# A weight conversion's negative step on GpSimd instead of ScalarE, and eight times it added on VectorE

## The chip, the core and the metric

The kernel runs on one core of a Trainium2 chip. The metric is the device time of one execution in microseconds (us); several runs are given by their median. Below, PE is TensorE, DVE is VectorE, ACT is ScalarE, POOL is GpSimd and SP is the engine that issues nearly all DMAs.

## The reference, cut to what matters

The program is an RWKV-6 attention block (4 batches, 8 heads, 768 tokens, head width 48) whose output goes through an MLP mixer. Only the mixer's four weights matter for this change:

```python
h = np.maximum(xt @ w_tok1, 0.0) @ w_tok2
u = x + h.transpose(0, 2, 1)
h2 = np.maximum(u @ w_ch1, 0.0) @ w_ch2
return (u + h2).astype(np.float32)
```

They are handed to the kernel as 64-bit words (the host only views them as such and lays them out), and the kernel makes float32 numbers of them from the 16-bit pieces of each word: it has to turn the top 16 bits into a power of two with its sign, and multiply the rest of the word by it.

## The kernel before

**Stages.** The work begins with the first batch's attention in three units (0, 1, 2; each covers 256 tokens of all heads), while the weights are loaded and converted. Then comes the first batch's mixer: the token product (`hidden`, L947), its way back (`back`, L958), turning x (`turn`, L969), the channel products `up` (L993) and `down` (L1004). The other three batches follow with their attention laid between the matmuls of the mixers.

**What orders the work.** Up to the first `back`, the order is written out by hand in one call of `strict` (L1094 to L1109). After that, `interleaved` merges streams of pieces by the string `ORDER`. `strict` chains the instructions of PE, DVE, ACT and SP, each engine in the order written. POOL is not chained: its instructions stand in the order in which the program made them, and each starts when its semaphores allow. Each engine works through its instructions in order, so one that waits holds up all behind it.

**The conversion.** There are twelve conversions, three of the token weights (`to_tok`; t0, t1, t2 below) and nine of the channel weights (`to_ch`; c0 to c8). Each takes 1024 words per partition, in seven steps that `convert` (L252) makes:

- `load` (L261): a DMA brings the words into one of four rooms (`raw`, `xT`, `z`).
- `positive` (L264), ACT: max(0, 8·top − 114688) over `top`, the highest 16 bits of each word, read with a step of four 16-bit numbers; written as int16 into `plus`.
- `negative` (L267), ACT: max(0, −8·top − 114688) into `minus`.
- `lead` (L270), DVE: `plus − minus`, a `tensor_sub` of two int16 tiles.
- `raise_two` (L273), DVE: the exponent's bits of that, into `minus` again.
- `put` (L277), DVE: rest of the word times the power of two, into the weights.
- `add` (L281), DVE: adds the leading part.

`plus` and `minus` lie in one of three pairs of rooms, so a later conversion's `minus` must wait for the `put` that reads the earlier one. All these tiles lie in SBUF.

**Around it.** The hand-written order puts conversions between the attention's steps. On DVE these are `ends` (L435, a scan), `begins` (L443, a scan), `keys` (L440), `queries` (L446), `own_put` (L458, reads PSUM) and `mask` (L327, a `copy_predicated` of PSUM data). On PE the third unit's `after` (L401) reads what its `mask` wrote. On ACT are the copies of states by the decay (L501), the range flags (L427), the attention's output copies (L407) and the copies of the turned x (L971). POOL makes a few constants at the start, and from the second batch on adds tiles of the mixer (L765).

Of the kernel before, what the change touches and what calls it, by code (L numbers as in the profile page):

```python
# [18 lines left out]
ALU = mybir.AluOpType  # L19
AF = mybir.ActivationFunctionType  # L20
# [6 lines left out]
UB = C // UC  # L27
NU = B * UB
A = H // 2
# [18 lines left out]
SHRINK = (1.0 - 1.0 / BASE) ** 2  # L48
LEAST, MOST = 2.0 ** -40, 2.0 ** 40
MID = 3 * G // 4 * SEG1  # L50
ORDER = (
    "888008088078808800000888484440800840804080880808804844088488400448088408008888080080884808884040488844488888084840880880"
    "808840880808084448484008800080858808005000458500505588854545558485085848785005080558505855588400558085800005606068606846"
# [12 lines left out]
def rwkv6_then_mixer(  # L66
# [25 lines left out]
    def behind(gate, f):  # L92

        def g():
            done = len(block.instructions)
            f()
            tc.add_manual_dep(block.instructions[done], ended[gate], wait, reason="time of issue")

        return g

    def strict(*fs):

        for f in fs:
# [82 lines left out]
    def load_part(i, n):  # L186
        for rows in (slice(0, 128),) if i < UB else (slice(0, D), slice(P, P + D)):
            sp.dma_start(rk_of(i)[rows, ts(n, COLS)], rk[i, n, rows, :])

    def load_rk(i):  # L190
        if i < NU:
            for n in (1, 0):
                load_part(i, n)
# [3 lines left out]
    def load_v(i):  # L197
        if i < NU:
            vs[i] = vpool.tile([128, UC, DM], f32, name="vt", tag=f"vt{i % 2}")
            b, j = divmod(i, UB)  # L200
            sp.dma_start(vs[i], v[b, ts(j, UC * 128), :].rearrange("(c p) e -> p c e", p=128))
# [50 lines left out]
    def convert(to, words, raw, room):  # L252

        word = raw_words[raw]
        rest = word.rearrange("p (n two) -> p n two", two=2)[:, :, 0]
        top = word.bitcast(i16).rearrange("p (n four) -> p n four", four=4)[:, :, 2]
        plus, minus = parts[room]
        leading, power = plus.bitcast(bf16), minus.bitcast(bf16)

        def load():  # L260
            sp.dma_start(word.bitcast(u16)[:, :words.shape[1]], words)  # L261

        def positive():
            act.activation(plus, top, AF.Relu, bias=rebias, scale=8.0)  # L264

        def negative():
            act.activation(minus, top, AF.Relu, bias=rebias, scale=-8.0)  # L267

        def lead():
            dve.tensor_sub(plus, plus, minus)  # L270

        def raise_two():
            dve.tensor_scalar(minus.bitcast(u16), plus.bitcast(u16), 0xFF80, None, op0=ALU.bitwise_and)  # L273

        def put():
            for dst, cols in to:
                dve.scalar_tensor_tensor(dst, rest[:, cols], 2.0 ** -36, power[:, cols], op0=ALU.mult, op1=ALU.mult)  # L277

        def add():
            for dst, cols in to:  # L280
                dve.tensor_add(dst, dst, leading[:, cols])  # L281

        return load, positive, negative, lead, raise_two, put, add
# [125 lines left out]
    def unit(i):  # L409
# [123 lines left out]
        def each(f, n):  # L533
            return [lambda m=m: f(m) for m in range(n)]

        return dict(ranges=each(ranges, 2), ends=ends, keys=keys, begins=begins, queries=queries, own_u=each(own_u, A),
                    own_gram=own_gram, copied=each(copied, UC), taken=each(taken, 3),
                    own_put=own_put, products=[lambda n=n: products(n) for n in range(3)], sums_put=sums_put,
                    tokens=tokens, gram=gram, mask=mask, carry=carry, before=before, seen=seen, after=after,
# [478 lines left out]
    def attention_pieces(i):  # L1018
# [6 lines left out]
        def piece(f, name, *ops):  # L1025
            return (i, name), f, ops
# [10 lines left out]
        loads = piece(lambda: load_rk(i + 1), "loads", ("Q", 8.0, last("before", "gram", "tokens")))  # L1037
        ends = piece(e["ends"], "ends", ("DVE", 2.6, last("small", "large", "by3", "w")))
        keys = piece(e["keys"], "keys", ("DVE", 1.25, k("ends") + last("loads")))
        small, large = (piece(e["ranges"][n], name, ("ACT", 1.4, k("ends"))) for n, name in enumerate(("small", "large")))  # L1040
        begins = piece(e["begins"], "begins", ("DVE", 2.35, k("ends")))
        tokens = piece(e["tokens"], "tokens", ("PE", 0.9, k("keys") + last("carry"), "k0", "k1"))
        copied = [piece(e["copied"][n], f"copied{n}", ("ACT", 0.6, k("tokens")), ("free", f"k{n}")) for n in range(2)]
# [31 lines left out]
    def interleaved(order, *streams):  # L1075
# [9 lines left out]
    raw_words.append(turned["xT"].rearrange("p m t -> p (m t)").bitcast(u32)[:, :4 * PIECE])  # L1085
    to_tok = conversion(("wtok1", "wtok2"), words_tok, rooms=lambda n: ((0, 1, 3)[n], n % 2))
    to_ch = conversion(("wch1", "wch2"), words_ch, rooms=lambda n: (n % 2, n % 2) if n else (2, 2))
    e0, e1, e2 = (unit(i) for i in range(UB))
    (_, p0, n0, lead0, two0, put0, add0), (_, p1, n1, lead1, two1, put1, add1), (_, p2, n2, lead2, two2, put2, add2) = to_tok
    _, p3, n3, lead3, two3, put3, _ = to_ch[0]  # L1090
    in_turn.update({pe.engine: None, dve.engine: None, act.engine: None, sp.engine: None})
    s0, s1, s2 = (e["updates"] for e in (e0, e1, e2))
    t0, t1, t2 = (e["scaled"] for e in (e0, e1, e2))
    strict(lambda: load_part(0, 1), masks, e0["ends"], e0["own_u"][0], e0["own_u"][1], e0["own_u"][2], e0["own_u"][3], e0["begins"],  # L1094
           lambda: load_part(0, 0), e0["keys"], lambda: load_part(1, 1), e0["own_gram"], lambda: load_v(0), e0["ranges"][0], lambda: load_w(1),
           e0["tokens"], e0["queries"], e1["own_u"][0], e1["own_u"][1], e0["copied"][0], lambda: load_w(2), e0["gram"], e1["ends"], e0["copied"][1],
           lambda: load_part(1, 0), e0["carry"], e1["own_u"][2], s0[0], e0["own_put"], e1["own_u"][3], e0["ranges"][1], t0[1], s0[1],
           behind(e0["tokens"], to_tok[0][0]), e1["begins"], behind(e1["ends"], lambda: load_part(2, 1)), e1["own_gram"], t0[2], e1["keys"],
           e2["own_u"][0], s0[2], e2["own_u"][1], e1["own_put"], t0[3], e1["tokens"], behind(e0["tokens"], lambda: load_part(2, 0)),
           e0["before"], e2["own_u"][2], e0["mask"], e1["copied"][0], p0, e0["seen"], s0[3], e2["own_u"][3], behind(t0[2], lambda: load_v(1)),  # L1100
           e2["ends"], e1["copied"][1], t1[0], e0["after"], e0["taken"][0], e1["carry"], n0, to_tok[1][0], s1[0], e1["queries"], e0["taken"][1],
           e2["keys"], lead0, t1[1], e2["own_gram"], two0, s1[1], e0["taken"][2], e2["own_put"], e2["tokens"], t1[2], put0, e2["copied"][0],
           s1[2], t1[3], e2["copied"][1], e1["gram"], s1[3], e1["before"], t2[0], p1, add0, lambda: load_v(2), e1["mask"], e2["carry"], e1["seen"],
           h[1], s2[0], h[0], e2["ranges"][0], e2["begins"], behind(t1[1], to_tok[2][0]), t2[1], n1, h[3], e2["queries"], s2[1], lead1, two1,
           e1["after"], t2[2], s2[2], put1, e2["gram"], behind(e1["gram"], to_ch[0][0]), h[2], e1["taken"][0], e1["taken"][1], t2[3], e1["taken"][2],
           behind(t2[3], lambda: load_w(3)), p2, add1, e2["mask"], lambda: load_v(UB), behind(e2["own_gram"], to_ch[1][0]), e2["before"], h[4],
           e2["seen"], n2, e2["after"], lead2, two2, h[5], e2["taken"][0], h[6], e2["taken"][1], put2, e2["taken"][2], h[7], h[8], p3,
           h[10], add2, n3, behind(e1["tokens"], to_ch[2][0]), lead3, two3, rectified[0], h[9], h[11], rectified[1], e1["ranges"][0], e2["ranges"][1], e1["ranges"][1],
           lambda: load_rk(3), put3, lambda: turned["back"](0))  # L1109

    six_banks.close()
    ps_g, ps_m = None, six_banks.enter_context(tc.tile_pool(name="ps_m", bufs=1, space=bass.MemoryType.PSUM))
# [2 lines left out]
    def single(steps, n):  # L1115

        load, positive, negative, lead, raise_two, put, add = steps
        k = lambda *names: tuple(("to", n, name) for name in names)
        last = lambda back, *names: tuple(("to", n - back, name) for name in names) if n > back else ()
        whole = [("load", load, ("Q", 5.0, last(2, "value", "minus"))), ("plus", positive, ("ACT", 1.15, k("load") + last(2, "put"))),  # L1120
                 ("minus", negative, ("ACT", 1.15, k("load") + last(2, "value"))), ("lead", lead, ("DVE", 0.69, k("plus", "minus"))),
                 ("two", raise_two, ("DVE", 0.35, k("lead"))), ("value", put, ("DVE", 1.23, k("two"))), ("put", add, ("DVE", 1.23, k("value")))]
        return [(("to", n, name), f, (op,)) for name, f, op in (whole[-1:] if n == 0 else whole[1:] if n <= 2 else whole)]

# [221 lines left out]
```

## Time and profile before

| | us |
|---|---|
| median of 3 runs | 479.33 (477.25 to 480.75) |
| the profiled execution | 478.31 |
| its span in the trace | 476.5 |

The profiled execution is 1.81 us longer than its span: that is what lies around the span. PE is busy for 459.1 us of the span, DVE for 344.6, ACT for 265.8 and POOL for 54.2. A row of a timeline gives the start and the length in us, the engine, the line, the operation, the tiles as out<-in with partitions x elements and types, the number of merged instructions, and in brackets the idle time before it with what ended it. A row that groups instructions gives the shortest, the median and the longest in ns. Busy time on an engine says what it did, not what the end of the program waited for; the chain of waits says that.

### The profile page before, as it was taken

How to read it: one execution, taken by the hardware profiler on the slowest of the kernel's cores; microseconds unless marked ns; L12 is line 12 of the kernel's file. 1: busy time of each engine (PE TensorE's matmuls, PEld its weight loads, DVE VectorE, ACT ScalarE, POOL GpSimd, SP SyncE). 2: the span in 40 equal slices, each digit the busy share in tenths (PEclk: the TensorE clock that was granted, in tenths of full speed). 3: DMA queues.
4: the chain of work that ended last, by engine and by line, in shares of the span. 5: the costliest groups of instructions: out<-in, count | busy, mean ns of one | idle time of the engine just before them, and what ended most of it. 6: DMA issues, size and time to landing. Idle time of an engine off the chain costs nothing.

```text
span 476.5 us, 12778 instructions
## 1 busy us (share of the span) xinstructions
PE 459.1 (96%) x5322; PEld 409.6 (86%) x5322; DVE 344.6 (72%) x495; ACT 265.8 (56%) x606; POOL 54.2 (11%) x58
## 2 busy tenths in 40 slices
PE   3899999999999999999999999999999999999996
PEld 2776588856797668999999999999999999999995
DVE  7998797679598877876897998685587885235341
ACT  6699876674678856453747385351837554134140
POOL 1000000000000001231302002130304003032130
PEclk9999999999999999999999999999999999999999
DMA  8865745573584556963888842754784513336331
GB/s 313 317 221 217 188 169 191 180 275 99 152 228 138 177 179 207 284 186 100 252 283 232 294 154 56 198 173 141 215 227 150 167 61 84 115 101 199 86 99 54
DMA packets 45055, 85.34 MB, mean 179 GB/s; under 512 B 4736, under 2 KB 37376, under 8 KB 44992
## 3 DMA queue, kind: packets, MB, share of 16 engines
q1 hardware_dynamic: 44704, 84.37, 56.3%
q8 instruction: 43, 0.70, 0.6%
q14 instruction: 20, 0.16, 0.1%
q10 hardware_dynamic: 288, 0.10, 0.1%
HBM read 72.65 MB, written 11.80 MB: 177 GB/s over the span
## 4 chain that ended last, share of the span: by engine, by line
PE 90%; ACT 4%; DVE 2%; DMA 2%; issue 1%; SPq 0%; DVEq 0%; ACTq 0%
PE bank L1004 10%; PE bank L772 8%; PE bank L779 8%; PE bank L774 8%; PE bank L790 8%; PE bank L792 8%; PE bank L791 8%; PE bank L993 7%; PE bank L667 3%; PE bank L989 3%; PE bank L726 3%; PE bank L315 2%; PE bank L401 2%; PE bank L380 2%; PE kv_ps L365 2%; PE bank L669 2%
## 5 line engine op out<-in xcount | busy, mean ns | idle before, releaser
L765 POOL TENSOR_TENSOR z_high<-z_high 128x384 fp32r<-128x384 f32 x48 | 52.9, 1107 | 406.7 <-DMA ring<-third 186.8
L754 ACT ACTIVATE z_high<-bank 128x384 fp32r<-128x384 f32 x48 | 23.5, 489 | 58.1 <-PE bank L779 57.7
L772 PE MATMUL bank<-x_forms,forms 128*128 128x384 f32 x216 | 50.3, 341 | 0.0
L779 PE MATMUL bank<-z_more,forms 128*128 128x384 f32 x216 | 50.1, 340 | 0.0
L774 PE MATMUL bank<-x_forms,ring 128*128 128x384 f32 x216 | 49.3, 337 | 0.0
L761 DVE SCALAR_TENSOR_TENSOR z_high<-bank,z_high 128x384 fp32r<-128x384 f32 x48 | 26.5, 554 | 31.4 <-ACT z_high L754 29.4
L1004 PE MATMUL bank<-wch,z 128*128 128x384 f32 x144 | 48.1, 488 | 0.0
L790 PE MATMUL bank<-forms,z_high 128*128 128x384 f32 x140 | 47.8, 342 | 0.0
L792 PE MATMUL bank<-forms,z_high 128*128 128x384 f32 x140 | 47.1, 337 | 0.0
L791 PE MATMUL bank<-ring,z_high 128*128 128x384 f32 x140 | 47.1, 337 | 0.0
L798 DVE SCALAR_TENSOR_TENSOR x<-bank,x 128x384 f32<-128x384 f32 x35 | 18.8, 553 | 39.0 <-PE bank L792 38.9
L1004 PEld LDWEIGHTS bank<-wch,z 128*128 128x128 f32 x144 | 26.8, 190 | 17.2
L501 ACT ACTIVATE before<-state,to_end 112x48 f32<-112x48 f32 x132 | 33.1, 324 | 13.0 <-DVE state L516 7.6
L779 PEld LDWEIGHTS bank<-z_more,forms 128*128 128x128 f32 x216 | 39.0, 188 | 0.1
L772 PEld LDWEIGHTS bank<-x_forms,forms 128*128 128x128 f32 x216 | 38.3, 188 | 0.5
L774 PEld LDWEIGHTS bank<-x_forms,ring 128*128 128x128 f32 x216 | 38.6, 188 | 0.0
L993 PE MATMUL bank<-xT,wch 128*128 128x256 f32 x144 | 32.0, 381 | 0.0
L993 PEld LDWEIGHTS bank<-xT,wch 128*128 128x128 f32 x144 | 27.0, 190 | 3.7
L757 ACT ACTIVATE z_high<-z_high 128x384 fp32r<-128x384 f32 x48 | 25.2, 525 | 3.5
L790 PEld LDWEIGHTS bank<-forms,z_high 128*128 128x128 f32 x140 | 26.3, 188 | 0.2
L791 PEld LDWEIGHTS bank<-ring,z_high 128*128 128x128 f32 x140 | 26.3, 188 | 0.0
L792 PEld LDWEIGHTS bank<-forms,z_high 128*128 128x128 f32 x140 | 26.3, 188 | 0.0
(243 smaller groups left out, 961.2 us busy)
## 6 DMA issues: line engine op xcount, KB each, us to landing
ring<-third SPq DMA_DIRECT2D x144, 192.0 KB, 3.4
raw<-in_words_ch_dram SPq DMA_DIRECT2D x8, 1023.8 KB, 4.8
rk<-in_rk_dram SPq DMA_DIRECT2D x36, 192.0 KB, 5.2
near<-in_near_dram SPq DMA_DIRECT2D x8, 768.0 KB, 5.0
w<-in_w_dram SPq DMA_DIRECT2D x10, 520.5 KB, 5.1
vt<-in_v_dram SPq DMA_DIRECT2D x12, 384.0 KB, 5.0
out_dram<-x SPq DMA_DIRECT2D x17, 192.0 KB, 2.8
third<-forms SPq DMA_DIRECT2D x12, 192.0 KB, 3.3
```

Source lines behind the costliest of these rows:

```text
L501: act.mul(t[:ROWS, a], state[bt, g][:ROWS, a], by_last(c, j)[:, a:a + 1])
L757: act.mul(z_form(jt, 2), z_form(jt, 0).bitcast(f32), 1.0 / BASE)
L761: dve.scalar_tensor_tensor(z_form(jt, 1), a, 0.0, z_form(jt, 0).bitcast(f32), op0=ALU.max, op1=ALU.subtract)
L765: pool.tensor_add(z_form(jt, 2), z_form(jt, 2).bitcast(f32), z_form(jt, 1).bitcast(f32))
L772: pe.matmul(a, up[m], xf(0)[:, m], start=m == 0, stop=False)
L774: pe.matmul(a, low[:, m], xf(1)[:, m], start=False, stop=False)
L779: pe.matmul(banks["a", jt], joint, xf(2)[:, m], start=False, stop=m == 2)
L790: pe.matmul(a, z[0], up, start=first, stop=False, skip_group_check=True)
L791: pe.matmul(a, z[1], held[bt, s, half, 1, jt], start=False, stop=False, skip_group_check=True)
L792: pe.matmul(a, z[2], joint, start=False, stop=last, skip_group_check=True)
L993: pe.matmul(ps, now["wch1"][:, jt // 4, m, ts(jt % 4, 128)], xT[:, m, ts(s, SEG)], start=(m == 0), stop=(m == DM // 128 - 1))
L1004: pe.matmul(ps, zs[s][:, jt, ts(n, 128)], now["wch2"][:, jt, :], start=(jt == 0), stop=(jt == NJ - 1))
```

## The change

`negative` becomes a `tensor_scalar` of POOL on the same `top`: the smaller of top and −14336, plus 14336. That is an eighth of what ACT made, with the other sign. `lead` becomes a `scalar_tensor_tensor` of DVE: `minus` times 8, plus `plus`. The numbers that come out are the same.

```diff
         def negative():
-            act.activation(minus, top, AF.Relu, bias=rebias, scale=-8.0)
+            pool.tensor_scalar(minus, top, -896.0 * 16, 896.0 * 16, op0=ALU.min, op1=ALU.add)
 
         def lead():
-            dve.tensor_sub(plus, plus, minus)
+            dve.scalar_tensor_tensor(plus, minus, 8.0, plus, op0=ALU.mult, op1=ALU.add)
...
-                 ("minus", negative, ("ACT", 1.15, k("load") + last(2, "value"))), ("lead", lead, ("DVE", 0.69, k("plus", "minus"))),
+                 ("minus", negative, ("POOL", 1.5, k("load") + last(2, "value"))), ("lead", lead, ("DVE", 0.69, k("plus", "minus"))),
```

The numbers in the last pair of lines are not used when the program is built, since `ORDER` is fixed. The rest of the diff writes the hand-made order as a string of names, `FIRST`, with the same steps in the same places, so that lines after L51 move down by 11 (and after L1100 by 7). L264, L267, L270, L273, L277 and L281 of before are L275, L278, L281, L284, L288 and L292 of the changed kernel. PE and SP keep their instructions in the same order.

On ACT the twelve `negative` steps leave their places and nothing else moves. This is ACT before, from c0's `positive` on, while PE makes the first batch's `back` (`h` is the hidden layer, `junk,flags` the range checks, `xT` the turned x):

```order
L264 ACTIVATE z_130<-z_129,rebias 128x1024
L267 ACTIVATE z_130<-z_129,rebias 128x1024
L950 ACTIVATE h_145<-h_ps 128x384 x2
L427 ACTIVATE junk,flags<-to_end_93,least 112x1041
L427 ACTIVATE junk,flags<-first,most 112x1041
L427 ACTIVATE junk,flags<-to_end_93,most 112x1041
L264 ACTIVATE raw<-raw,rebias 128x1024
L267 ACTIVATE raw<-raw,rebias 128x1024
L971 COPY xT<-bank_875 128x3x128
L971 COPY xT<-bank_877 128x3x128
```

And the same place now:

```order
L275 ACTIVATE z_130<-z_129,rebias 128x1024
L961 ACTIVATE h_145<-h_ps 128x384 x2
L438 ACTIVATE junk,flags<-to_end_93,least 112x1041
L438 ACTIVATE junk,flags<-first,most 112x1041
L438 ACTIVATE junk,flags<-to_end_93,most 112x1041
L275 ACTIVATE raw<-raw,rebias 128x1024
L982 COPY xT<-bank_875 128x3x128
L982 COPY xT<-bank_877 128x3x128
```

The step between `positive` and the copies is gone, so the copies stand right behind c1's `positive`.

On POOL, the queue between the constants at the start and the mixer's additions was empty, and now holds the twelve steps. POOL now:

```order
L229 MEMSET flags 128x24
masks.py:197 MEMSET ident 128x128
L232 MEMSET strictly 128x64
masks.py:199 ISA
masks.py:199 AFFINE_SELECT ident<-ident 128x128
L234 AFFINE_SELECT strictly<-strictly 64x64 x2
L278 TENSOR_SCALAR raw<-raw 128x1024 x2
L278 TENSOR_SCALAR raw<-xT 128x1024
L278 TENSOR_SCALAR z_130<-z_129 128x1024
L278 TENSOR_SCALAR raw<-raw 128x1024 x8
L776 TENSOR_TENSOR z_high<-z_high 128x384 x48
```

Before, the row of the additions (L765 there) stood directly behind the second AFFINE_SELECT. Each of the twelve now waits for its words and for its room alone.

On DVE no row moves; `lead` changes its kind. From t0's `lead` to t1's, DVE now:

```order
L281 SCALAR_TENSOR_TENSOR raw<-raw 128x1024
L284 TENSOR_SCALAR raw<-raw 128x1024
L469 TENSOR_TENSOR at_92<-gram,u_rows 128x1024
L288 SCALAR_TENSOR_TENSOR wtok_124<-raw 128x1024
L292 TENSOR_TENSOR wtok_124<-wtok_124,raw 128x1024
L338 COPY_PREDICATED first<-before_it,gram 128x1024
L454 SCALAR_TENSOR_TENSOR x<-x,starts 112x1041
L457 TENSOR_TENSOR first<-first,x 112x1024
L281 SCALAR_TENSOR_TENSOR raw<-raw 128x1024
```

The first and the last row were TENSOR_TENSOR (L270) before; what stands between them is the same (the scan `begins`, L454 here, is printed as SCALAR_TENSOR_TENSOR).

More of the change, by code (lines that the diff above doesn't have):

```diff
@@ L50 @@
 MID = 3 * G // 4 * SEG1
+FIRST = (
[9 rows of a table added]
+)
 ORDER = (
@@ L534, in each @@
             return [lambda m=m: f(m) for m in range(n)]
-        return dict(ranges=each(ranges, 2), ends=ends, keys=keys, begins=begins, queries=queries, own_u=each(own_u, A),
+        return dict(small=lambda: ranges(0), large=lambda: ranges(1), ends=ends, keys=keys, begins=begins, queries=queries, own_u=each(own_u, A),
                     own_gram=own_gram, copied=each(copied, UC), taken=each(taken, 3),
@@ L1039, in attention_pieces @@
         keys = piece(e["keys"], "keys", ("DVE", 1.25, k("ends") + last("loads")))
-        small, large = (piece(e["ranges"][n], name, ("ACT", 1.4, k("ends"))) for n, name in enumerate(("small", "large")))
+        small, large = (piece(e[name], name, ("ACT", 1.4, k("ends"))) for name in ("small", "large"))
         begins = piece(e["begins"], "begins", ("DVE", 2.35, k("ends")))
@@ L1087, in rwkv6_then_mixer @@
     to_ch = conversion(("wch1", "wch2"), words_ch, rooms=lambda n: (n % 2, n % 2) if n else (2, 2))
-    e0, e1, e2 = (unit(i) for i in range(UB))
-    (_, p0, n0, lead0, two0, put0, add0), (_, p1, n1, lead1, two1, put1, add1), (_, p2, n2, lead2, two2, put2, add2) = to_tok
-    _, p3, n3, lead3, two3, put3, _ = to_ch[0]
+    first = {i: unit(i) for i in range(UB)}
     in_turn.update({pe.engine: None, dve.engine: None, act.engine: None, sp.engine: None})
-    s0, s1, s2 = (e["updates"] for e in (e0, e1, e2))
@@ L1093, in rwkv6_then_mixer @@
[L1093 to L1109, printed above, removed]
@@ new lines, in rwkv6_then_mixer @@
+    named = {"masks": masks, "rk3": lambda: load_rk(3), "back0": lambda: turned["back"](0)}
+    named.update({f"h{n}": f for n, f in enumerate(h)})
+    named.update({f"relu{n}": f for n, f in enumerate(rectified)})
+    for kind, weights in (("t", to_tok), ("c", to_ch[:3])):
+        for n, steps in enumerate(weights):
+            named.update({f"{kind}{n}.{name}": f for name, f in zip(("load", "plus", "minus", "lead", "two", "value", "sum"), steps)})
+    for i, e in first.items():
+        named.update({f"{'rk'[n]}{i}": lambda i=i, n=n: load_part(i, n) for n in range(2)})
+        named.update({f"w{i + 1}": lambda i=i: load_w(i + 1), f"v{i}": lambda i=i: load_v(i)})
+        for name, made in e.items():
+            name = {"own_u": "own", "own_gram": "own", "own_put": "put", "scaled": "by", "updates": "up"}.get(name, name)
+            named.update({f"{i}.{name}{n}": f for n, f in enumerate(made)} if isinstance(made, list) else {f"{i}.{name}": made})
@@ L1111, in rwkv6_then_mixer @@
+    named["v3"] = lambda: load_v(UB)
+    for name in FIRST.split():
+        name, _, gate = name.partition("<")
+        strict(behind(named[gate], named[name]) if gate else named[name])
     six_banks.close()
```

9 rows, old and new, of the table FIRST are left out of this document.

## The prediction

> **What bounds the kernel now.** First the page's busy times, then busy times by stage, to see where a weight conversion can matter at all.
>
> ```profile
> PE 459.1 (96%) x5322; PEld 409.6 (86%) x5322; DVE 344.6 (72%) x495; ACT 265.8 (56%) x606; POOL 54.2 (11%) x58
> ...
> core 0: us, PE busy (x) PEld busy (x) DVE busy (x) ACT busy (x) POOL busy (x), PEclk, DMA share, GB/s
> 20.00:59.00 39.00, 36.58 (x765) 25.51 (x764) 32.48 (x38) 35.61 (x81) 0.00 (x0) 1.00 0.68 221
> 59.00:125.00 66.00, 66.00 (x590) 49.97 (x591) 54.96 (x68) 41.90 (x83) 0.00 (x0) 1.00 0.48 168
> ```
>
> From 59 us on PE is never idle up to 125 us: a conversion costs nothing there as long as its weights and keys come in time. Before 59 us the first batch's attention and mixer go hand to hand between PE, ACT (91% busy) and DVE (83%); whatever delays a hand-over moves the start of PE's full stretch, and so the end. POOL does nothing there. So the sum is the shift of PE at 59 us, and what later waits add to it.
>
> Then DVE's timeline from t0's `lead` to the third unit's `mask`, and what PE has behind that:
>
> ```profile
> 25.64 1.21 DVE L440 TENSOR_TENSOR first<-first 112x1024 f32<-112x1024 f32 x1
> 27.07 0.69 DVE L270 TENSOR_TENSOR raw<-raw 128x1024 int16<-128x1024 int16 x1 [0.22 <-ACT raw L267]
> 27.80 0.43 DVE L273 TENSOR_SCALAR raw<-raw 128x1024 uint16<-128x1024 uint16 x1
> 28.52 1.23 DVE L458 TENSOR_TENSOR at<-gram,u_rows 128x1024 f32<-128x1024 f32 x1 [0.30 <-PE gram L315]
> 29.66 1.22 DVE L277 SCALAR_TENSOR_TENSOR wtok<-raw 128x1024 f32<-128x1024 uint32 x1
> 30.91 1.22 DVE L281 TENSOR_TENSOR wtok<-wtok,raw 128x1024 f32<-128x1024 f32 x1
> 32.06 1.30 DVE L327 COPY_PREDICATED first<-before_it,gram 128x1024 f32<-128x1024 uint8 x1
> 33.26 2.31 DVE L443 TENSOR_TENSOR_SCAN x<-x,starts 112x1041 f32<-112x1041 f32 x1
> 35.60 1.23 DVE L446 TENSOR_TENSOR first<-first,x 112x1024 f32<-112x1024 f32 x1
> 37.40 0.69 DVE L270 TENSOR_TENSOR raw<-raw 128x1024 int16<-128x1024 int16 x1 [0.57 <-ACT raw L267]
> ...
> 41.00 1.30 DVE L327 COPY_PREDICATED at<-before_it,gram 128x1024 f32<-128x1024 uint8 x1
> ...
> 42.55 1.15 PE L401 MATMUL y_ps<-vt,at 64*64 64x48 f32 x64
> ```
>
> The `mask` at 41.00 ends at 42.30, and PE's `after`, which reads it, starts at 42.55: DVE sets this hand-over. DVE's idle times since 25.64 are few: 0.22, 0.30 and 0.57.
>
> **The change part by part.** *Removed from ACT*: twelve instructions of 1.2 us. What ACT's queue gains is worth something where ACT is the last to be waited for. The clearest place is c1, shortly before 59 us:
>
> ```profile
> 54.46 1.21 ACT L267 ACTIVATE raw<-raw,rebias 128x1024 int16<-128x1024 int16 x1
> ...
> 55.70 0.69 DVE L270 TENSOR_TENSOR raw<-raw 128x1024 int16<-128x1024 int16 x1 [1.83 <-ACT raw L267]
> ...
> 58.02 0.55 DVE L960 TENSOR_TENSOR x<-x,bank 128x384 f32<-128x384 f32 x1
> ...
> 58.72 0.52 PE L969 MATMUL bank<-ident,x 128*128 128x128 f32 x3 [0.59 <-ACT raw L267]
> ```
>
> DVE had waited 1.83 us for L267, and behind this `lead` stands L960, whose x the last early `turn` (58.72) needs. Without L267 in the queue, `lead` can start when L264 ends, 1.1 us earlier.
>
> *Added on DVE*: `lead` as a scalar_tensor_tensor. The trace has none on int16 pairs. The bounds are the 0.69 us that the plain subtraction takes and the 1.22 us of L277, a scalar_tensor_tensor over as many elements. I take 1.22, since it is the same instruction: +0.53 us each, twelve times. At c1 that leaves 1.1 − 0.5 = 0.6 us gained.
>
> *Added on POOL*: `tensor_scalar` over 1024 int16, which the trace does not have either. The nearest rows are its one-input and its two-input operations:
>
> ```profile
> L223 POOL TENSOR_SCALAR_AFFINE_SELECT strictly<-strictly x2: 232/234/237, 1.4 to 1.7; 64x64 f32<-64x64 f32 x2
> ...
> masks.py:199 POOL TENSOR_SCALAR_AFFINE_SELECT ident<-ident x1: 293/293/293, 1.2 to 1.2; 128x128 f32<-128x128 f32 x1
> ...
> L765 POOL TENSOR_TENSOR z_high<-z_high x48: 1000/1014/2002, 188.7 to 460.6; 128x384 fp32r<-128x384 f32 x48
> ```
>
> One input: 59 ns more for 64 more elements, 0.92 ns each, on a base of 0.175 us: 1.1 us for 1024. Two inputs: (1.014 − 0.175) / 384 = 2.2 ns each: 2.4 us. It has one input, but two arithmetic steps and int16 on both sides; I take 1.5 us, a third of the way from the nearer end, and keep 1.1 and 2.4.
>
> [...]
>
> *The collision.* POOL and DVE do not run freely beside each other:
>
> ```profile
> 191.28 1.28 DVE L488 TENSOR_TENSOR at<-bank,strictly 128x512 f32<-128x512 f32 x2
> 191.51 1.02 POOL L765 TENSOR_TENSOR z_high<-z_high 128x384 fp32r<-128x384 f32 x1 [0.28 <-DVE z_high L761]
> ...
> 210.26 1.32 DVE L473 COPY_PREDICATED at<-diagonal,sums 128x1024 f32<-128x1024 uint8 x1
> 210.51 1.91 POOL L765 TENSOR_TENSOR z_high<-z_high 128x384 fp32r<-128x384 f32 x1 [0.55 <-DVE z_high L761]
> 211.47 1.78 DVE L713 TENSOR_TENSOR spare<-spare 128x768 fp32r<-128x768 f32 x1
> ...
> L713 DVE TENSOR_TENSOR spare<-h_room,spare x1: 945/945/945, 213.9 to 213.9; 128x768 fp32r<-128x768 f32 x1
> ```
>
> POOL's addition came while L473 ran, and took 1.91 us instead of 1.01: it waited until L473 was nearly done. L713, next on DVE, took 1.78 instead of 0.95: it ends at 213.25, so its own work began at 212.30, just before POOL's end at 212.42. One excludes the other, and POOL, having waited, goes ahead of DVE's next. So a `negative` of 1.5 us can hold DVE up by 1.5 − 0.13 = 1.37 us each time. L473 and L713 take all their inputs from SBUF. L488, which reads a PSUM bank, ran beside an addition that took its usual 1.02 us; so I let L327 and L458, which read PSUM as well, run on beside POOL.
>
> [...]
>
> Words land here (issue, then the time to landing):
>
> ```profile
> 18.54 0.46 SPq L261 DMA_DIRECT2D raw<-in_words_tok_dram  x1
> 28.45 0.33 SPq L261 DMA_DIRECT2D xT<-in_words_tok_dram  x1
> 31.75 0.33 SPq L261 DMA_DIRECT2D z<-in_words_ch_dram  x1
> ...
> raw<-in_words_tok_dram SPq DMA_DIRECT2D x1, 1023.8 KB, 7.3
> xT<-in_words_tok_dram SPq DMA_DIRECT2D x1, 1023.8 KB, 4.8
> z<-in_words_ch_dram SPq DMA_DIRECT2D x1, 1023.8 KB, 5.0
> ```
>
> That is 25.8 for t1, 33.2 for t2 and 36.8 for c0, and POOL takes each as soon as it can, without regard to when DVE needs it. DVE's queue, step by step:
>
> 1. t1's `negative` waits for L440 (to 26.85) and holds the port from 26.7 to 28.1. t0's `lead` starts at 28.1 instead of 27.07: +1.0.
> 2. This `lead` is 0.53 longer: +1.55. The idle 0.30 before L458, and its spacing, take up 0.4: +1.15.
> 3. t2's `negative` runs from 33.2, mostly beside L327; L443 waits 0.1: +1.25.
> 4. c0's `negative` comes at 36.7, as L443 ends, and L446 waits for 1.2 more: +2.5. The 0.57 idle before t1's `lead`, a wait for an L267 that is gone, takes up 0.65: +1.8.
> 5. t1's `lead` is 0.53 longer: +2.4 at the `mask`, and so at PE's `after`.
>
> From there PE carries +2.4; at c1 it gets 0.6 back: +1.8 at 59 us. Later DVE falls further behind, by the port and by 0.53 per conversion, and two pieces of slack run out:
>
> ```profile
> 66.82 1.17 DVE L440 TENSOR_TENSOR rk<-rk,to_end 112x1024 f32<-112x1024 f32 x1
> ...
> 70.73 0.93 PE L345 MATMUL bank<-ident,rk 112*128 112x112 f32 x8
> ...
> 121.64 1.23 DVE L446 TENSOR_TENSOR rk<-rk,w 112x1024 f32<-112x1024 f32 x1
> ...
> 124.55 1.11 PE L315 MATMUL bank<-rk 48*64 48x64 f32 x62
> ```
>
> L440's keys are done 2.7 us before PE wants them; DVE is then 1.8 + 0.5 (c2's `lead`) + two blocks of 1.2 = 4.7 late: PE goes to +2.0. L446's queries are 1.7 us early at 124.55 while DVE is some 4.1 late: +2.4.
>
> **Sum**: +2.4 (to 42.55) − 0.6 (c1) + 0.6 (late) = +2.4 us. The profiled execution would take 478.3 + 2.4 = 480.7; it was 1.0 under the median, so the median becomes 479.33 + 2.4 = **481.7 us**.
>
> How it moves with POOL's price: each 0.1 us above 1.5 costs 0.3 by 42.55 (three `negative` steps in DVE's way) and up to 0.6 from the six after 59 us (c3 to c8), since DVE's free time there, 66.0 − 54.96 = 11.0 us, is already spent by seven longer `lead` steps (3.7) and six blocks (8.2). So 2.0 us gives about +6.9 and 2.4 about +10.5. Below 1.5 the late 0.6 vanishes and step 3 is free: at 1.1 us it is +1.0.
>
> **The rivals.** *DVE becomes the bound*: with a `negative` of 1.8 us or more (+5.1), DVE is late past every slack up to 125 us, and the time is above 484; at 2.0 us 486.2. For it: 2.4 us is a POOL row, and DVE already has only 11 us free. Against it: one input is nearer to the 1.1 us row. Chance 0.26.
>
> [...] Chance 0.12.
>
> *ACT's queue was the real bound before 59 us* (it is the busier engine there), and its lighter load lets the units run closer: over 4.8 us faster would need four places like c1, and I find one. Chance 0.03. That the change does not do what it says can be left out: the steps have left ACT's queue.
>
> **How the numbers follow.** The forecast, a small loss within 1%, has 0.59; with the case without collision, 0.71 lies within 1% (474.5 to 484.1), which is about what a measurement of this kernel can tell from no change. Slower by over 1%: 0.26; faster: 0.03. The range goes from 478.5, just under the case without collision, to 487.5, a `negative` of about 2.1 us.
>
> **What would show it.** In the changed profile: L278 on POOL near 1.5 us where nothing is in its way, longer after a DVE instruction with SBUF operands; DVE's L281 at 1.22 us, and L451, L457, L292 lengthened by up to 1.4 us when POOL got there first; PE's `after` (L412 there) at about 44.9 instead of 42.55, and `up` starting at 60.9 instead of 59.1. I am wrong if L278 takes 2 us or more, if DVE's rows keep their lengths beside it, or if PE starts `up` before 59 us.

## The result, and the profile after

The changed kernel takes 484.33 us (median of four runs, 483.37 to 487.21); before took 479.17 beside it. The ratio is 1.013, with a 95% interval of 1.010 to 1.016: about 6 us slower. Two later repeats gave 1.0122 (1.0082 to 1.0162) and 1.0131 (1.0102 to 1.0160). The forecast was 481.7; the range held the time, but the likeliest case was wrong: what came is a loss of more than 1%.

First the page's busy times and the busy times by stage of the profiled execution (483.98 us, span 482.3):

```profile
PE 460.5 (95%) x5322; PEld 409.9 (85%) x5322; DVE 358.5 (74%) x495; ACT 253.6 (53%) x594; POOL 104.8 (22%) x70
...
core 0: us, PE busy (x) PEld busy (x) DVE busy (x) ACT busy (x) POOL busy (x), PEclk, DMA share, GB/s
20.00:62.00 42.00, 37.92 (x768) 26.64 (x767) 39.14 (x39) 29.70 (x76) 24.28 (x6) 1.00 0.66 208
62.00:128.00 66.00, 63.52 (x440) 47.11 (x439) 58.25 (x66) 32.82 (x69) 24.49 (x6) 1.00 0.47 165
```

Twelve steps have added 50.6 us to POOL's busy time, 4.2 each where 1.5 was assumed; that includes POOL's waits for DVE (a step takes 3.66 us with DVE idle, in e9). The stretch from 62 to 128 us, in which PE had no idle time before, now has 2.5 us of it.

The early part of DVE's queue, and POOL's rows beside it. The columns are start, length, engine, line, operation:

```profile
25.32 4.15 POOL L278 TENSOR_SCALAR raw<-raw 128x1024 int16<-128x1024 int16 x1 [2.73 <-DMA raw<-in_words_tok_dram]
34.75 5.46 POOL L278 TENSOR_SCALAR raw<-xT 128x1024 int16<-128x1024 int16 x1 [5.28 <-DMA xT<-in_words_tok_dram]
40.17 3.89 POOL L278 TENSOR_SCALAR z<-z 128x1024 int16<-128x1024 int16 x1
...
25.80 2.17 DVE L451 TENSOR_TENSOR first<-first 112x1024 f32<-112x1024 f32 x1
27.89 1.21 DVE L281 SCALAR_TENSOR_TENSOR raw<-raw 128x1024 int16<-128x1024 int16 x1
29.13 0.62 DVE L284 TENSOR_SCALAR raw<-raw 128x1024 uint16<-128x1024 uint16 x1
...
36.75 1.95 DVE L457 TENSOR_TENSOR first<-first,x 112x1024 f32<-112x1024 f32 x1
...
40.52 2.10 DVE L288 SCALAR_TENSOR_TENSOR wtok<-raw 128x512 f32<-128x512 uint32 x2
...
38.98 1.02 PE L412 MATMUL y_ps<-vt,first 64*64 64x48 f32 x54 [1.34 <-issue]
...
45.18 1.15 PE L412 MATMUL y_ps<-vt,at 64*64 64x48 f32 x64 [0.50 <-DVE at L338]
```

The lead is 1.21 us, as assumed. L451 was 1.21 us and is 2.17: POOL, which began just ahead of it, kept it out for 0.95 us, but not for POOL's 4.15. The next lead (27.89) has two inputs in SBUF and runs at its usual length while POOL is still busy until 29.47. So it goes at L457 (0.72 longer) and L288 (0.81 longer). PE's third `after` comes at 45.18 instead of 42.55, and what it waits for last is DVE's `mask`; the stall of 1.34 us ahead of 38.98, for which the profile shows no cause, was over by then.

Then the late part, c6 and c8 of the changed kernel:

```profile
91.47 1.23 DVE L281 SCALAR_TENSOR_TENSOR raw<-raw 128x1024 int16<-128x1024 int16 x1 [1.55 <-POOL raw L278]
...
93.07 2.26 DVE L457 TENSOR_TENSOR rk<-rk,w 112x1024 f32<-112x1024 f32 x1
95.25 1.21 DVE L288 SCALAR_TENSOR_TENSOR wch<-raw 128x1024 f32<-128x1024 uint32 x1
...
92.93 3.91 POOL L278 TENSOR_SCALAR raw<-raw 128x1024 int16<-128x1024 int16 x1 [1.49 <-DMA raw<-in_words_ch_dram]
102.08 3.72 POOL L278 TENSOR_SCALAR raw<-raw 128x1024 int16<-128x1024 int16 x1 [5.24 <-DMA raw<-in_words_ch_dram]
...
105.84 1.23 DVE L281 SCALAR_TENSOR_TENSOR raw<-raw 128x1024 int16<-128x1024 int16 x1 [4.00 <-POOL raw L278]
...
108.96 1.22 DVE L292 TENSOR_TENSOR wch<-wch,raw 128x1024 f32<-128x1024 f32 x1
...
95.47 1.16 PE L326 MATMUL bank<-rk 48*64 48x64 f32 x64 [1.14 <-DVE rk L457]
...
110.24 4.78 PE L1015 MATMUL bank<-wch,z 128*128 128x384 f32 x14 [1.15 <-DVE wch L292]
```

and the same places before, which the prediction did not look at:

```profile
87.48 0.69 DVE L270 TENSOR_TENSOR raw<-raw 128x1024 int16<-128x1024 int16 x1 [2.99 <-ACT raw L267]
...
89.68 1.22 DVE L277 SCALAR_TENSOR_TENSOR wch<-raw 128x1024 f32<-128x1024 uint32 x1
...
98.25 0.69 DVE L270 TENSOR_TENSOR raw<-raw 128x1024 int16<-128x1024 int16 x1 [1.87 <-ACT raw L267]
...
100.83 1.23 DVE L281 TENSOR_TENSOR wch<-wch,raw 128x1024 f32<-128x1024 f32 x1
...
95.89 1.23 ACT L264 ACTIVATE raw<-raw,rebias 128x1024 int16<-128x1024 int16 x1 [2.07 <-DMA raw<-in_words_ch_dram]
```

These rows make a chain. c8's words go into the room that c6's `put` has read. From there, before and after: c6's `put` ends at 90.90 and 96.46 (+5.56); c8's words come 4.99 and 5.62 us later (+0.63); its lead starts 2.36 and 3.76 us after them (+1.40, POOL instead of two steps of ACT); the lead is 0.53 longer; the rest takes 3.1 in both. c8's `add` ends at 102.06 and 110.18, 8.12 us later. Counting PE's instructions, the matmul that waits at 110.24 is the one that ran at 105.20 before: it had 3.1 us in hand, and is 5.04 late. c6's own +5.56 is again its lead, 3.99 later (87.48 and 91.47; it had waited for ACT, and now waits for POOL), the lead's 0.54 and 1.04 for L457, which c7's `negative` (92.93 on POOL) held up.

Following PE's instructions in this way, PE is 0.47 us late at 27.6 (before any conversion's lead can have reached it), 2.6 at the third `after`, 2.4 when `up` starts, and then 3.7 at the queries of 95.47, 5.0 at c8's weights, 5.8 and 6.6 at the next unit's keys and queries. So 2.4 us are lost before 62 us, 0.5 of them older than the conversions, and 4.2 between 62 and 128.

### The profile page after: what moved, and what is told of

It is laid out like the page before. It is cut to its first block, busy times and chain, and to the rows that moved or that the text cites. A ratio compares the mean times of both kernels' runs of the same rounds, so it can differ in the third digit from the quotient of the medians.

```text
span 482.3 us, 12803 instructions
## 1 busy us (share of the span) xinstructions
PE 460.5 (95%) x5322; PEld 409.9 (85%) x5322; DVE 358.5 (74%) x495; ACT 253.6 (53%) x594; POOL 104.8 (22%) x70
## 4 chain that ended last, share of the span: by engine, by line
PE 74%; DVE 14%; DMA 6%; issue 2%; POOL 2%; ACT 1%; SPq 1%; DVEq 0%; ACTq 0%; POOLq 0%
PE bank L783 8%; PE bank L790 8%; PE bank L785 8%; PE bank L801 8%; PE bank L803 8%; PE bank L802 8%; PE bank L1015 4%; DMA raw<-in_words_ch_dram 3%; PE bank L678 3%; PE bank L737 3%; PE bank L1000 3%; DVE raw L281 2%; PE bank L412 2%; PE bank L391 2%; DMA w<-in_w_dram 2%
## 5 line engine op out<-in xcount | busy, mean ns | idle before, releaser
L765 ACT ACTIVATE z_high<-bank 128x384 fp32r<-128x384 f32 x48 | 23.5, 490 | 57.3 <-PE bank L790 56.8
L278 POOL TENSOR_SCALAR raw<-raw 128x1024 int16<-128x1024 int16 x10 | 40.9, 4093 | 48.3 <-DMA raw<-in_words_ch_dram 22.5
L801 PEld LDWEIGHTS bank<-forms,z_high 128*128 128x128 f32 x140 | 26.3, 188 | 0.2
```

The lines of the kernel that those rows point to most:

```text
L278: pool.tensor_scalar(minus, top, -896.0 * 16, 896.0 * 16, op0=ALU.min, op1=ALU.add)
L801: pe.matmul(a, z[0], up, start=first, stop=False, skip_group_check=True)
```

## The experiments

The first theory: the early loss is POOL's hold on DVE and the longer lead; the late loss is the 3.7 us that POOL takes until its result is there. Rival A: the late loss is DVE's added work, wherever it lies. Times below are the ratio to before, turned into us with the median of before (478.2 to 478.5), with its interval. "PE's late loss" is how much more PE is behind at the instruction that before ran at 127 us than at that of 61 us, in the profiled execution.

**The lead alone** (e1)

```diff
-            pool.tensor_scalar(minus, top, -896.0 * 16, 896.0 * 16, op0=ALU.min, op1=ALU.add)
+            act.activation(minus, top, AF.Relu, bias=eighth, scale=-1.0)
...
-            dve.scalar_tensor_tensor(plus, minus, 8.0, plus, op0=ALU.mult, op1=ALU.add)
+            dve.scalar_tensor_tensor(plus, minus, -8.0, plus, op0=ALU.mult, op1=ALU.add)
```

> The negative step stays on ScalarE (in an eighth of its size), lead becomes the scalar_tensor_tensor of the change, POOL does nothing more than before. Theory (the early loss is POOL's hold of DVE, the late loss is the 3.8 us that a negative takes on POOL): the longer lead costs 0.53 us each, of which slack takes most up; PE's third `after` starts 0.3 to 0.8 us later than before, nothing is added between 62 and 128 us, and the time is +0.3 to +1.5 us against before. Rival A (the late loss comes from VectorE's added work, seven leads of 0.53 us after 59 us): PE waits for VectorE between 90 and 125 us here too, +3 us or more. Rival B (the early loss is the longer lead's): +1.5 us or more at PE's third `after`.

Measured: 1.0043 (1.0024 to 1.0061), +2.1 us, more than the 1.5 expected at most. In the trace PE loses 0.4 us up to the third `after` and 0.6 more by 59 us; 1.2 us stood there before the first lead, where the granted clock was 0.57 (18 to 30 us), so the leads explain 1.0 us of this trace. PE's late loss is 0.0: twelve longer leads do not make it by themselves.

**Early and late half** (e3, e4)

```diff
+        on_pool = n < 6
...
+            if on_pool:
+                pool.tensor_scalar(minus, top, -896.0 * 16, 896.0 * 16, op0=ALU.min, op1=ALU.add)
+            else:
+                act.activation(minus, top, AF.Relu, bias=rebias, scale=-8.0)
```

and lead accordingly; n counts the conversions from t0 (0) to c8 (11). e4 has `n >= 6`.

> The first six conversions (t0 to t2, c0 to c2) as in the change, the last six (c3 to c8) as before. Theory: the early loss as in the change, +2.3 to +2.9 us at PE's third `after` and +2.0 to +2.6 where `up` starts; after that at most +0.7 us, so +2 to +3.3 us in all, and PE has no wait of 1 us for VectorE between 90 and 125 us. Rival A: VectorE's lateness carried from the early part already makes half of the late loss, +4.5 us or more in all. Rival C (PE's stall of 1.4 us at 37 us is noise of one execution): it is not there, and the third `after` is +1.5 us or less late.

> The first six conversions as before, the last six (c3 to c8) as in the change. Theory: nothing moves up to 62 us; then VectorE waits up to 5 us at two leads for POOL, later weights and keys come late, and PE loses 3 to 4.5 us between 90 and 125 us: +3 to +4.5 us in all. Rival A: VectorE has only three longer leads in its way before 105 us and enters the stretch on time, so its slack of about 2 us takes half of it: +2 us or less.

Measured: early 1.0037 (1.0018 to 1.0056), +1.8 us; late 1.0084 (1.0059 to 1.0109), +4.0 us. Together 5.8, which is the change. PE's late loss is 0.0 with the early half and 3.4 with the late one, so rival A, which wanted 4.5 or more of the early half and 2 or less of the late one, misses both. Rival C is right about the stall at 37 us, which is not there, but the third `after` is still 1.7 us later than PE already was at 27.6.

**POOL without the longer lead** (e7)

```diff
-            dve.scalar_tensor_tensor(plus, minus, 8.0, plus, op0=ALU.mult, op1=ALU.add)
+            dve.tensor_max(plus, plus, minus)
```

> POOL makes all twelve negative steps as in the change; lead is the larger of plus and minus, a plain operation of two int16 tiles, which drops the negative weights (their signs and sizes come out wrong). So the change without its longer lead. Theory: holds and the 3.8 us stay: +1.3 to +2.2 us at PE's third `after`, +3 to +4 us more by 125 us, together +4 to +5.5 us. Rival A (VectorE's longer leads make the late loss): at most +1.5 us more after 62 us, together +3 us or less.

This lead leaves out the negative weights; a plain addition in its place (e2) gave no time. Measured: 1.0050 (1.0027 to 1.0073), +2.4 us. That is well below the theory's 4 to 5.5 and inside what rival A allows (3 or less). PE's late loss is 3.0 in the trace, which speaks against rival A, but the profiled execution is the slowest of nine, 483.8 us: c8's words landed 6.8 us after c6's `put`, and its lead waited 5.8 us for POOL. So this run alone doesn't settle between the two. The lead alone costs 2.1, POOL alone 2.4, both 6. That looks as if each used slack that the other then lacks; the intervals are too wide for these three times to show it.

**The holds alone** (e6)

```diff
+            if n >= 6:
+                unused = word.bitcast(i16).rearrange("p (n four) -> p n four", four=4)[:, :, 3]
+                pool.tensor_scalar(unused, top, -896.0 * 16, 896.0 * 16, op0=ALU.min, op1=ALU.add)
             act.activation(minus, top, AF.Relu, bias=rebias, scale=-8.0)
```

> The kernel before, with ScalarE's negative and the plain subtraction in all twelve; for c3 to c8 POOL runs the same tensor_scalar as in the change in addition, on the same words when they land, into their unused fourth 16-bit piece, which nobody reads. So VectorE has POOL's holds, but neither a longer lead nor a wait for POOL's result. Theory (the late loss is the time until POOL's result is there): +0 to +1 us. Rival A' (the late loss is what POOL's holds take from VectorE): +2.5 us or more, with PE waiting for VectorE between 90 and 125 us.

Measured: 1.0063 (1.0040 to 1.0087), +3.0 us, PE's late loss 3.1. The first theory falls: nobody waits for POOL's result here, and a late loss nearly as large is there. How much of the change's own late loss is holds, this run doesn't say: its POOL step is longer than the real one (5.2 us; it writes with a step of 8 bytes), and its holds came at telling places:

```profile
89.84 2.07 DVE L291 TENSOR_SCALAR raw<-raw 128x1024 uint16<-128x1024 uint16 x1
91.83 2.11 DVE L464 TENSOR_TENSOR rk<-rk,w 112x1024 f32<-112x1024 f32 x1
...
103.31 2.40 DVE L291 TENSOR_SCALAR raw<-raw 128x1024 uint16<-128x1024 uint16 x1
```

L291, the raising to a power, takes 0.43 us otherwise, L464 takes 1.22. The first two stand between c6's lead and its `put`, the third between c8's lead and its `put`: on the chain above. c8's `add` ends 6.3 us later than before, and PE's matmul that reads it is 6.3 − 3.1 = 3.2 late. The same subtraction fits wherever PE waited for c8: 6.1 and 3.0 in e4, 6.4 and 3.3 in e7, 8.1 and 5.0, 7.1 and 4.0, 6.4 and 3.3 in three executions of the change.

So the theory became: the late loss runs along the **chain of rooms** (c4's `put`, c6's words, lead, `put`, c8's words, lead, `add`, PE), and whatever lies on it counts, be it lead, hold or wait, once its 3.1 us are spent.

**c8, or c6 and c8, back on ACT** (e10 is the changed kernel beside them; e11 has `on_pool = n != 11`, e12 has `on_pool = n not in (9, 11)`)

> The changed kernel once more, for the two that follow: +5 to +6.5 us against before; PE's down matmuls wait at 110 us for c8's add, as in its first trace.

> The change, but the last conversion (c8) as before. Theory, new after e6 and e7: the late loss runs along the chain of rooms, c4's put, c6's words, c6's lead, c6's put, c8's words, c8's lead, c8's add, PE's down; on it c8 costs 1.4 us for POOL's result and 0.53 for the lead. PE's wait for c8's add shrinks by 1.3 to 1.9 us, until the wait for unit 3's queries sets the end: +3.3 to +4.7 us against before. Rival A (VectorE's added work counts wherever it lies): only c8's 0.53 us goes, since its POOL step held no VectorE instruction up: within 0.6 us of the changed kernel.

> The change, but c6 and c8 as before. Theory of the chain of rooms: c6's lead waited for POOL until 91.67 us, so c6 gains up to 1.4 us for POOL's result, 0.53 for the lead and up to 0.8 for a hold, and c8 another 1.9: c8's add is late by no more than PE already is: +2.2 to +3.2 us against before, that is, no late loss. Rival A (VectorE's added work counts wherever it lies): of six late conversions four are left, so two thirds of the late loss: +4.3 us or more.

Measured: the change +5.8 us, without c8 1.0055 (1.0027 to 1.0082), +2.6, without c6 and c8 1.0031 (1.0006 to 1.0056), +1.5. PE's late loss is 3.9, 0.9 and 0.0. One conversion of twelve carries about 3 of the 5.8 us (3.2 here, 2.9 in the repeat below), though its POOL step held nothing up: rival A, by which it would have been within 0.6, falls. Both times are lower than expected (3.3 to 4.7 and 2.2 to 3.2): c8 is worth more than the 1.3 to 1.9 that the chain's theory gave it.

**c8 alone on POOL, and c8's lead against POOL's result** (e13 has `on_pool = n == 11`; e14 is the change with the two lines of e1 at n = 11)

> The kernel before, with c8 alone as in the change. Theory of the chain of rooms: c8's add comes 1.4 (POOL's result) plus 0.53 (lead) = 1.9 us later, and PE's down asked for it 3.1 us after its end: no wait, -0.4 to +0.5 us. Rival (c8's step costs its 3.2 us by itself): +2 us or more.

> The change, but c8's negative on ScalarE (an eighth of its size, other sign) with the longer lead kept; the eleven others on POOL. Theory: POOL's result is what c8 waits for; the lead's 0.53 us fits into what is left: as e11, +2 to +3.7 us against before. Rival (the longer lead decides at c8): +4.7 us or more, near the changed kernel.

Measured: e13 1.0019 (1.0001 to 1.0037), +0.9 us, a little over what was expected, with this row:

```profile
98.93 1.23 DVE L290 SCALAR_TENSOR_TENSOR raw<-raw 128x1024 int16<-128x1024 int16 x1 [3.59 <-POOL raw L284]
```

DVE waits 3.59 us for POOL, nearly as long as in the change (4.00), and PE loses only 0.7. The longest wait in a trace can cost next to nothing; the step costs about 3 us only behind the other eleven.

e14 gave 1.0106 (1.0077 to 1.0135), +5.1 us, as if the lead decided; but its trace has a late loss of 1.6 only. Its granted clock (the column after the busy times) is low early on, during the token product (L968 there):

```profile
core 0: us, PE busy (x) PEld busy (x) DVE busy (x) ACT busy (x) POOL busy (x), PEclk, DMA share, GB/s
30.00:42.00 12.00, 11.77 (x391) 8.78 (x388) 11.86 (x10) 10.36 (x33) 9.77 (x3) 1.00 0.50 177
42.00:54.00 12.00, 10.03 (x88) 6.16 (x82) 10.33 (x11) 3.72 (x8) 4.99 (x2) 0.72 1.02 322
...
46.77 6.90 PE L968 MATMUL h_ps<-x,wtok 128*128 128x384 f32 x14
```

Before, the same 14 matmuls took 5.57 us from 43.62 on, with a gap of 0.53 in them. PE is 1.6 us more behind at 59 us than at its third `after` there, where the change's traces have it 0.3 to 1.1 less behind. That explains this execution, not the median of four. So the three were run side by side:

> e14's kernel again: c8's negative on ScalarE, the longer lead kept. If c8 waits for POOL's result (e14's trace): +3 to +4.3 us against before, 1.5 us or more below the changed kernel in this call. If the longer lead decides (e14's time): within 0.8 us of the changed kernel.

> e11's kernel again: +2 to +3.3 us against before; by either theory 2 us or more below the changed kernel in this call.

> The changed kernel in the same call: +5 to +6.2 us against before.

Measured: the change 1.0131 (1.0102 to 1.0160), +6.3; POOL's result gone at c8 1.0095 (1.0078 to 1.0113), +4.5; the lead gone too 1.0071 (1.0048 to 1.0095), +3.4. PE's late loss is 4.2, 2.5 and 1.1. The second is 1.7 below the first, as POOL's result asks for (1.5 or more). All three times lie 0.1 to 0.2 us above their forecasts. PE's waits from 60 to 130 us, in this order (line, what it waited for, us in total, times, longest; L336 and L337 are L326 of the changed kernel, the product that reads the queries):

```profile
PE bank L1015 <- DVE wch L292: 1.9, 1, 1.9
```

```profile
PE bank L336 <- DVE rk L467: 1.7, 2, 1.1
```

```profile
PE bank L337 <- DVE rk L468: 0.5, 1, 0.5
```

The wait for c8's weights goes with POOL's result; what is left are queries. The first of these traces, the changed kernel's, has only that one wait, as its granted clock was 0.50 just behind it (columns as in the table above):

```profile
109.00:112.00 3.00, 3.00 (x6) 1.53 (x5) 2.59 (x4) 3.00 (x5) 0.00 (x0) 0.50 0.01 3
...
108.47 6.48 PE L1015 MATMUL bank<-wch,z 128*128 128x384 f32 x14 [1.89 <-DVE wch L292]
```

These 14 matmuls took 4.78 us in the first trace of the change. The late loss of 4.2 hardly hangs on it: the next unit's queries were ready at 129.25 and PE came for them at 129.56.

Both parts count; by the traces (3.9 to 4.2, then 1.6 and 2.5, then 0.9 and 1.1) POOL's result is about 2 us and the lead 1, by the times of these three 1.7 and 1.1, by e14's time 0.7 and 2.5. A finer split stays open.

**POOL's price and its hold** (e5, e9: single instructions)

> Not the kernel: a list of single POOL instructions with VectorE idle, then six POOL instructions beside a stream of one kind of VectorE instruction; the output is zeros. Theory: `negative` as the change has it takes 3.7 to 3.9 us alone; its price is that of arithmetic on 16-bit integers by POOL, so it stays above 3 us when the input lies without a step, and float32 to float32 is well below (1.1 to 2.4 us). Rival by step: the input's step of 8 bytes makes it, and without a step it falls below 2.2 us. Rival by arithmetic: one step of arithmetic instead of two halves it. Beside VectorE (theory, from the changed kernel): additions of two SBUF tiles get one row longer by 0.9 to 1.1 us per POOL instruction, the 16-bit bitwise steps wait until POOL has ended, additions with one input in PSUM keep their length. Rival (POOL keeps VectorE out for its whole length): 3 us or more in one row of additions.

> Not the kernel: single POOL instructions with VectorE idle, then `negative` beside seven streams of VectorE instructions, one kind each, every engine in a fixed order; the output is zeros. After e5, where the streams met POOL in no fixed order: copy 1.1 us, one arithmetic step 2.8 to 3.0, two steps 3.6 to 3.7, for int16 with and without a step and for float32 alike. Theory (POOL keeps VectorE out only while it reads): of seven additions of two SBUF tiles one is 0.7 to 1.0 us longer than 1.22, the others not; the same for the two leads and for the scaled product; of the bitwise steps one is up to 3.7 us longer or ends with POOL; additions with a PSUM input stay at 1.2. Rival (POOL keeps VectorE out for its whole 3.7 us): one row of 4 us or more in every stream without PSUM.

In e5 the streams met POOL in no fixed order, and only its prices can be used; e9 has the same ones in clean rows. Groups of e9 (shortest, median and longest in ns). L59 is `negative`, with step and without; L91 and L93 are one arithmetic step on int16 and on float32; L97 adds two tiles, L99 copies:

```profile
L59 POOL TENSOR_SCALAR m<-word x11: 3620/3662/3683, 19.9 to 118.4; 128x1024 int16<-128x1024 int16 x11
...
L91 POOL TENSOR_SCALAR m<-word x2: 2763/2767/2771, 34.8 to 37.7; 128x1024 int16<-128x1024 int16 x2
...
L93 POOL TENSOR_SCALAR ga<-gb x2: 2764/2764/2764, 40.4 to 43.2; 128x1024 f32<-128x1024 f32 x2
...
L97 POOL TENSOR_TENSOR ga<-ga,gb x2: 2337/2337/2337, 53.5 to 55.9; 128x1024 f32<-128x1024 f32 x2
...
L99 POOL COPY ga<-gb x2: 1036/1038/1040, 58.3 to 59.4; 128x1024 f32<-128x1024 f32 x2
...
L68 DVE TENSOR_TENSOR a<-a,b x14: 1221/1226/2141, 60.6 to 78.8; 128x1024 f32<-128x1024 f32 x14
...
L71 DVE TENSOR_TENSOR c<-c,pair x7: 1211/1220/1221, 80.0 to 87.5; 128x1024 f32<-128x1024 f32 x7
...
L74 DVE SCALAR_TENSOR_TENSOR p<-q,p x7: 1218/1225/2136, 88.7 to 97.2; 128x1024 int16<-128x1024 int16 x7
...
L80 DVE TENSOR_SCALAR p<-q x16: 426/427/1339, 108.1 to 116.7; 128x1024 uint16<-128x1024 uint16 x16
```

Neither the step of 8 bytes nor int16 makes the price: it is the arithmetic. A copy is 1.04 us, one arithmetic step 2.77, two 3.66. For float32 e5 had expected 1.1 to 2.4 us; that was wrong. DVE's streams show the hold. Additions with an input in PSUM (L71) keep their length; in the streams from SBUF the longest row is 0.91 us longer than the median (additions L68, the new lead L74, bitwise steps L80). So POOL keeps them out for 0.91 us at its start and not for its 3.66. Of the bitwise steps (L80; 534 ns on average, 427 at the median) a second one, across POOL's end, is longer by 0.8, as L284 at 29.13 in the changed kernel, across POOL's end at 29.47, takes 0.62 us instead of 0.43; neither waits out the whole of POOL's step, as had been expected of them both times.

**What is left of ACT's relief** (e8 and e15 have `on_pool = n == 4`, c1 alone; e16 `n in (4, 5)`)

> Only c1's negative on POOL with the longer lead, all others as before. Theory: c1's words have landed long before its lead, so POOL's 3.8 us are over in time; lead starts 1 us earlier, is 0.53 us longer and VectorE is held once for 1 us: -0.6 to +0.7 us, nothing late. Rival (any use of POOL beside VectorE costs): +1 us or more.

> The kernel before, with c1 alone as in the change, for the second time: -0.5 to -1.8 us against before.

> The kernel before, with c1 and c2 as in the change. ScalarE's queue loses a second step before it turns x for `up`, but c1 already let that go ahead: theory, no more than 0.3 us beyond c1 alone, and c2's lead is 0.53 longer without anybody waiting: -0.5 to -1.8 us against before. Rival (each step taken from ScalarE before 59 us is worth 1 us): -1.8 to -2.8 us.

Measured: c1 0.9971 (0.9951 to 0.9991) and 0.9991 (0.9977 to 1.0004), −1.4 and −0.4 us; c1 and c2 1.0012 (0.9995 to 1.0029). In both traces of c1 alone PE gains 1.3 us between the third `after` and `up`, but only 0.5 of it between the last `back` and `up`, where c1 lies. Most of the rest is a stall in the token product, for which the profile gives no cause; this is its row in the trace of before:

```profile
45.38 3.81 PE L947 MATMUL h_ps<-x,wtok 128*128 128x384 f32 x11 [0.53 <-issue]
```

It comes and goes whatever the kernel: e13, with c1 as before, gains 0.5 us there too. Between the last `back` and `up`, PE gains 0.3 to 0.8 us in all 13 traces with c1 on POOL, e16's among them (0.5), nothing in e4, e6 and e13, and loses 0.5 in e1. So the relief is real and about 0.5 us, as much as PE's wait of 0.59 at 58.72 before. As a faster kernel c1 alone is not established, since the second interval takes in no change, and the gain of 0.5 to 1.8 us expected of c1 and c2 did not come.

## Why the prediction was wrong, point by point

- **What bounds the kernel**: right. The loss is PE's shift at the hand-overs before 62 us and a few waits after.
- **ACT's relief at c1**, −0.6: right; −0.5 between the last `back` and `up` in the first trace of the changed kernel, and −0.5 there where c1 was changed alone.
- **The lead at 1.22 us**: right, 1.20 to 1.23.
- **The chain on DVE up to the `mask`**, +2.4: right in size, in part by luck. +2.6 in the trace, of which 0.5 is older. Within it, t1's `negative` did not wait for L440 but began ahead of it and held it up by 0.95; t2's `negative` was not beside L327 but waited for the scan and held L457 up by 0.7, and c0's took 0.8 from L288 in place of 1.2 from L446. Three holds of 0.7 to 0.95 happen to make about what one of 1.0, one of 0.1 and one of 1.2 were to make. With c1, +1.8 was expected at `up`; the trace has 2.4, of which 0.5 is older, and the first six conversions alone cost 1.8 (e3).
- **POOL's price**, 1.5 us with bounds of 1.1 and 2.4: wrong, 3.66, with the step of 8 bytes and without (e9). The nearest rows misled: an affine_select as the row for one input, an addition as that for the dearer case. A single-input step with arithmetic (2.77) is dearer than the addition of two tiles (2.34). This was also a sign of being wrong that the prediction had named, L278 at 2 us or more.
- **The hold**, all of POOL's instruction but 0.13: wrong, 0.91 at its start (e9), 0.7 to 1.0 in the kernel. The row that it rested on could not tell the two apart: there POOL's addition took 1.01 us without its wait, and L713 came 0.83 late. The two errors worked against each other: by the prediction's slope of 0.9 us per 0.1, a step of 3.66 us would have cost some 19 us more, far outside the range, so that the range held the time is luck. No run shows a port that POOL and DVE share, by which the sum counts in its first step and in the late part; what the runs showed in its place is this hold, of DVE's rows that read SBUF alone, while additions with an input in PSUM kept their 1.22 us (e9). The bitwise step, at 0.43 us and with its one input in SBUF, was held by 0.91 and 0.8 of POOL's 3.66 us (e9), and by 1.64 and 1.97 in e6 (2.07 and 2.40 against 0.43). The case without collision, which lies at the lower end of the range, did not come.
- **"Later DVE falls further behind … and two pieces of slack run out", +0.6**: this is the step that failed; it measured 3.9 to 4.2 us. It looked for DVE's lateness only at the attention's keys and queries. The keys at 70.73 were not late at all; the queries of 124.55 were, and cost 0.8. The lateness went into the chain of rooms, where each lead, hold and wait delays the next load, and c8's `add` came 8.1 us later against 3.1 in hand. The trace of before had the rows: c8's `add` at 100.83, and c6's `put`, which frees the room, 5 us ahead of c8's words.
- **The rival "DVE becomes the bound"**: its time was right (above 484, by 0.3 us) and its condition held (a step of 1.8 us or more), its reason only in part. DVE still idles (58.25 busy of 66 us); what binds is one chain through it.

## What to carry to other kernels

Price a moved step at the consumer with the least in hand, and follow buffers as well as data: where a room is reused, a delay at one step becomes the next load's delay, and it adds up around the loop. Slack that each part of a change fits into alone can be overrun by the parts together, so undo single links of the chain, and do not read the cost of a wait from its length. Where a trace has no row for an operation, a nearby operation is no bound (here the bounds were 1.1 and 2.4 us, and 3.66 came); an experiment with that one instruction is.

## What the runs showed of the hardware

- POOL on 128x1024 elements: copy 1.04 us, addition of two tiles 2.34, tensor_scalar with one step 2.77 and with two 3.66, alike for int16 and float32 (e9); written with a step of 8 bytes, two steps take 5.07 (e5) and, in two single rows, 5.15 and 5.19 (e6).
- A scalar_tensor_tensor of int16 tiles takes 1.22 us on DVE where a plain subtraction takes 0.69 (e9).
- The granted clock differed between executions for 3 to 12 us at a time (0.57 between 18 and 30 us in e1, 0.72 between 42 and 54 us in e14, 0.50 between 109 and 112 us in e19; 1.00 in the first profiles of before and after). Where PE was the bound there, 14 matmuls took 1.3 and 1.7 us longer (6.90 us in e14 against 5.57 before, and 6.48 in e19 against 4.78 in the first trace of the change), so a shift between two single traces of this kernel is safe only within one stage.
